# Two of four row blocks turned by VectorE and DMAs in the prologues of an attention and Fourier kernel

## The chip, the cores and the metric

The kernel runs on one core of a Trainium2 chip. The metric is the device time in microseconds of one execution. Before the change the median of three runs is 2447.65 us, the lowest 2446.1 and the highest 2448.53. A profiled execution of the same kernel took 2448.28 us. Its span, from the first to the last instruction, is 2446.5 us; all times inside the trace count from the span's start. The granted clock of TensorE was 0.998 of full speed over the span.

## The reference

The input x has 2048 rows (tokens) of 640 values in f32. Two kinds of block alternate, twice each, and each adds its result to x. An attention block normalizes every row, forms queries, keys and values with one 640 x 1920 matrix, runs 32 heads of 20 columns over all 2048 tokens with softmax, and multiplies with a 640 x 640 matrix. A Fourier block normalizes every row and takes the real part of a two-dimensional discrete Fourier transform, written as products with cosine and sine matrices.

```python
q, k, v = (x @ wqkv).reshape(B, S, 3, H, Dh) ...        # of the normalized x
p = softmax(einsum("bhqd,bhkd->bhqk", q, k) * Dh ** -0.5)
o = einsum("bhqk,bhkd->bhqd", p, v) ... @ wo
x = x + A(layernorm(x)); x = x + B(layernorm(x))         # and both once more
```

## The kernel before, in words

The kernel is written for the five engines with a schedule by hand: the order in which the code issues instructions is the order on each engine's queue. An engine works through its queue strictly in order, and a waiting instruction holds up all that stand behind it. SyncE (SP) and GpSimd (POOL) each have a queue of DMAs too. Tiles live in named pools: a tile that takes the place of an earlier one of the same tag waits until that one has been read.

There are two layers, each one attention block and one Fourier block. Each layer begins with a *prologue* (`Qkv.prologue`), and it is only this stage that the change touches. In it the rows of x are normalized, turned so that the 640 features lie on the partitions, and the first products are made from them: one 128-column chunk of queries, one of keys, and half of the value columns. After the prologue the attention proper begins, which holds most of the time.

The 2048 rows come in 16 tiles of 128 tokens. The prologue loads them in pairs, `k` = 0 to 7 (`load`, lines 148 to 153), and works in four *blocks* of 512 tokens, `tb` = 0 to 3; block `tb` holds the pairs 2 `tb` and 2 `tb` + 1. The steps of a block are these:

- `stats` (line 155): VectorE's statistics of a pair through `moments` (lines 114 to 129), and GpSimd's two small operations that make a scale and a bias of them (lines 127 and 128).
- `norm` (line 158): ScalarE applies these with `normed` (lines 131 and 132), in place.
- `turn` (lines 166 to 185): TensorE transposes the block against an identity, 4 tiles of tokens by 5 chunks of 128 features (`ND` is 5), into the PSUM tiles `ptr`. For each chunk, `split` (lines 85 to 91) makes the tile `xt` of two halves: ScalarE copies `ptr` into the high half, rounded to the type of TensorE's products; VectorE subtracts, which leaves the rest as the low half.
- the products of the block for the query and the key chunk, 15 matmuls each (`product`, through line 103: per chunk the high half, the low half, and the high half with the weights' low part), and `keep` (lines 200 to 225), which copies a product out, splits it the same way into `hl`, squares it for a bound, and has GpSimd write it to memory (`scrq`, `scrk`, line 224).
- `norms` (line 227), one small matmul `pn` and a maximum over it.
- `own` (line 339), four times: 15 matmuls make the values of one token tile (`pv`), and ScalarE copies them to `v` (line 265).

The loop over the blocks stands at the end of `prologue`. It is staggered: in block 0 the rows of block 2 are loaded, its statistics made and block 1's rows normalized. The values of block 0 are made ahead of `turn(1)`. In blocks 1 and 2 the next block is turned ahead of the values, so that ScalarE and VectorE split the chunks while TensorE works on `pv`. PSUM has eight banks, which the prologue's tiles take in turn.

On SyncE's queue stand, in order, the loads of x, a few small loads of `attention.setup` (line 495), the loads of the first queries (`qload`, lines 522 and 523), a load of weights (`fetch`, line 191) and those of the first keys (`kload`, lines 508 and 509). They serve the attention that follows, the weights a chunk of it. In the second layer the first block's rows are not loaded: `take` (line 285) normalizes them out of tiles of the Fourier block.

Of the kernel before, what the change touches and what calls it, by code (L numbers as in the profile page):

```python
# [5 lines left out]
F32 = mybir.dt.float32  # L6
F32R = mybir.dt.float32r
# [8 lines left out]
S, D, H, DH = 2048, 640, 32, 20  # L16
# [3 lines left out]
ND = D // 128  # L20
# [19 lines left out]
def mha_fnet_kernel(ctx, tc, x_in, wqk, wv, wo, seq, hid, nat_seq, nat_hid, out):  # L40
# [44 lines left out]
    def split(hl_h, hl_l, src, vector=False):  # L85

        if vector:
            V.tensor_copy(hl_h, src)  # L88
        else:
            A.activation(hl_h, src, AF.Copy)  # L90
        V.tensor_tensor(hl_l, src, hl_h.bitcast(F32), op=OP.subtract)  # L91
# [39 lines left out]
    def normed(dst, x, rs, i):  # L131
        A.activation(dst, x, AF.Identity, scale=rs[:, 0, i:i + 1], bias=rs[:, 1, i:i + 1])
# [5 lines left out]
    class Qkv:  # L138
        def __init__(s, L, src):
            s.L, s.src = L, src  # L140
            s.xn, s.xt, s.rs, s.v, s.sq = {}, {}, {}, {}, {}
            s.scr = {qk: dr.tile([D, 2, S], F32, name=f"scr{qk}_{L}") for qk in "qk"}
            s.shift = {n: dr.tile([H, 2, c], F32, name=f"shift{n}_{L}") for n, c in (("b", 512), ("m", S))}
            s.n = 1
            s.made, s.raw, s.silent = set(), {}, False


        def load(s, k):

            s.xn[k] = (s.first if k % 4 < 2 else s.room)(f"x{k % 4}", [2, D], F32, "xa")  # L150
# [15 lines left out]
        def turn(s, tb, wait=False):  # L166

            def transpose(p, i, dc):
                PE.transpose(p[:, i * 128:(i + 1) * 128],
                             s.xn[2 * tb + i // 2][:, i % 2, dc * 128:(dc + 1) * 128], ident)  # L170

            ps = [s.bank([128, 512], "ptr") for _ in range(ND if wait else 0)]
            for i in range(4 if wait else 0):
                for dc in range(ND):
                    transpose(ps[dc], i, dc)
            for dc in range(ND):
                if wait:
                    p = ps[dc]
                else:
                    p = s.bank([128, 512], "ptr")  # L180
                    for i in range(4):
                        transpose(p, i, dc)
                x = s.xtp(f"xt{tb}_{dc}", [2, 512], F32R, "xt")
                s.xt[tb, dc] = [x[:, 0], x[:, 1]]
                split(x[:, 0], x[:, 1], p)

        def fetch(s, c, room=None, tag="wraw", wait=False):
            s.raw[c] = (room or s.fill)(tag, [ND, 128], F32, "wraw")
# [83 lines left out]
        def begin(s, first, kq, vals, room, given):  # L272


            s.first, s.room, s.given, s.w = first, room, given, {}
            for k in range(2):
                if given:
                    s.raw[k * ND] = given.wraw[k]
                else:
                    s.load(k)  # L280
            s.wvraw = [vals(f"v{NT - 1 - dc}", [HD], F32, "wvraw") for dc in range(ND)]
            if given:
                s.load_values()

        def take(s, k):

            s.xn[k] = s.first(f"x{k}", [2, D], F32, "xa")
            for i in range(2):
                normed(s.xn[k][:, i], s.given.x[2 * k + i][:, 0], s.given.next[k], i)

# [4 lines left out]
        def prologue(s, vals, xt, fill, att):  # L295
# [39 lines left out]
            def later(tb, k, f):  # L335
                if tb + 2 < NB:
                    f(2 * tb + 4 + k)

            def own(tb, n, between=None):
                t = 4 * tb + n  # L340
                p = s.bank([128, HD], "pv")
                for dc in range(ND):
                    for f in s.value(p, t, dc):
                        f()
                    if between and dc == 1:
                        between()
                s.own(p, t, 0, False)

            for tb in range(NB):

                sq, late, last = {}, tb == 0, tb == NB - 1
                if late:
                    for k in range(2):
                        later(tb, k, s.load)
                for k in (1, 0) if last else (0, 1):
                    p = s.bank([128, 512], "pqk")
                    for dc in range(ND):
                        for f in s.product(p, s.w[k], tb, dc):
                            f()
                    sq[k] = s.keep(p, k * ND, tb, False, (room, fill)[k])  # L360
                    if late:
                        s.stats(2 + k)
                        continue
                    later(tb, k, s.stats)
                if late:
                    for n in range(4):
                        own(tb, n)
                        if n < 2:
                            s.norm(2 + n)
                            later(tb, n, s.stats)  # L370
                if tb == 0:
                    att.setup()
                elif tb == 1:
                    for t in range(NT - ND, NT):
                        ones(t)
                if tb + 1 < NB:
                    s.turn(tb + 1)
                    for k in range(2):
                        later(tb + 1, k, s.load)
                for k in range(1 if last else 0, 2):  # L380
                    later(tb, k, s.norm)
                    s.norms(s.bank, k * ND, tb, sq[k])
# [1261 lines left out]
```

## Time and profile before

| what | us |
|---|---|
| median of three runs | 2447.65 |
| lowest and highest | 2446.1, 2448.53 |
| the profiled execution | 2448.28 |
| its span | 2446.5 |
| TensorE busy in the span | 2423.7 |
| ScalarE busy | 2114.9 |
| VectorE busy | 996.3 |
| GpSimd busy | 530.7 |

In the profile PE is TensorE's matmuls, PEld its loads of weights, which run beside matmuls, DVE is VectorE, ACT is ScalarE, POOL is GpSimd and SP is SyncE; an engine's name with a q is its queue of DMAs. A group `xt<-ptr` writes the tile `xt` from the tile `ptr`. "L103" is line 103 of the kernel. A line like `29.43 2.56 ACT L90 ACTIVATE xt<-ptr ... x5` in a view in order of time means: from 29.43 us on, for 2.56 us, ScalarE ran five instructions of line 90. Its instructions overlap a little, so that the spacing from one to the next is shorter than one instruction's length. Brackets at the end of a line say how long the engine had been idle before it and what ended the wait.

### The profile page before, as it was taken

How to read it: one execution, taken by the hardware profiler on the slowest of the kernel's cores; microseconds unless marked ns; L12 is line 12 of the kernel's file. 1: busy time of each engine (PE TensorE's matmuls, PEld its weight loads, DVE VectorE, ACT ScalarE, POOL GpSimd, SP SyncE). 2: the span in 40 equal slices, each digit the busy share in tenths (PEclk: the TensorE clock that was granted, in tenths of full speed). 3: DMA queues.
4: the chain of work that ended last, by engine and by line, in shares of the span. 5: the costliest groups of instructions: out<-in, count | busy, mean ns of one | idle time of the engine just before them, and what ended most of it. 6: DMA issues, size and time to landing. Idle time of an engine off the chain costs nothing. (4 is left out here: it accounts for less than half of the span.)

```text
span 2446.5 us, 43831 instructions
## 1 busy us (share of the span) xinstructions
PE 2423.7 (99%) x16320; PEld 1167.8 (48%) x16320; DVE 996.3 (41%) x2250; ACT 2114.9 (86%) x2428; POOL 530.7 (22%) x1036
## 2 busy tenths in 40 slices
PE   8999999999999999999999999999999999999998
PEld 7644444443333332339885444454433333333496
DVE  6244442234343333428753444323433332333275
ACT  6699998899999999995457999988999999999862
POOL 2022211112212212115421212211111211222143
PEclk9999999999999999999999999999999999999999
DMA  5324231223232225318552332312221322252265
GB/s 186 101 88 127 83 111 53 77 69 111 73 95 90 87 89 164 98 38 293 196 181 96 112 102 86 117 54 70 78 82 57 93 63 69 57 153 79 77 240 198
DMA packets 128226, 262.63 MB, mean 107 GB/s; under 512 B 29936, under 2 KB 54288, under 8 KB 128004
## 3 DMA queue, kind: packets, MB, share of 16 engines
q1 hardware_dynamic: 89412, 159.89, 20.2%
q0 software_dynamic: 38592, 99.85, 12.8%
q8 instruction: 131, 2.15, 0.4%
q14 instruction: 91, 0.75, 0.1%
HBM read 175.29 MB, written 84.31 MB: 106 GB/s over the span
## 5 line engine op out<-in xcount | busy, mean ns | idle before, releaser
L547 ACT ACTIVATE e<-psc 128x1024 f32<-128x1024 f32 x2048 | 1917.3, 1060 | 108.8 <-PE psc L544 98.2
L555 PE MATMUL acc<-e,v 128*32 128x512 f32 x8192 | 1030.0, 600 | 0.4 <-DVE of L562 0.4
L544 PE MATMUL psc<-stq,stk 62*128 62x512 f32 x4096 | 746.7, 445 | 1.9 <-ACT e L547 0.5
L544 PEld LDWEIGHTS psc<-stq,stk 62*128 62x128 f32 x4096 | 334.2, 184 | 704.8 <-ACT e L547 567.7
L555 PEld LDWEIGHTS acc<-e,v 128*32 128x32 f32 x8192 | 211.0, 108 | 407.2 <-issue 369.7
L103 PE MATMUL pqk<-xt,wqk 128*128 128x512 f32 x1200 | 319.1, 407 | 0.4 <-DVE xt L91 0.4
L576 POOL DMA_DIRECT2D o<-oh x256 | 131.8, 523 | 825.0 <-DVE oh L571 813.1
L88 DVE CAST hl<-pqk 128x512 fp32r<-128x512 f32 x64 | 44.3, 692 | 603.7 <-PE pqk L103 603.7
L103 PEld LDWEIGHTS pqk<-xt,wqk 128*128 128x128 f32 x1200 | 213.2, 188 | 83.5 <-issue 39.5
L103 PE MATMUL pv<-wv,xt 128*128 128x320 f32 x960 | 151.7, 313 | 0.0
L103 PEld LDWEIGHTS pv<-wv,xt 128*128 128x128 f32 x960 | 141.0, 188 | 13.5 <-issue 9.7
L562 DVE STREAM_TRANSPOSE of<-acc 128x512 f32<-128x512 f32 x64 | 45.8, 715 | 225.3 <-PE acc L555 225.3
L576 POOL DMA_DIRECT2D o<-ot x256 | 128.2, 509 | 1.1 <-issue 0.8
L224 POOL DMA_DIRECT2D scrk<-hl x40 | 27.7, 693 | 412.3 <-DVE hl L91 251.9
L224 POOL DMA_DIRECT2D scrq<-hl x40 | 28.3, 707 | 405.5 <-DVE hl L91 239.9
L96 PE MATMUL py<-wo,o 128*128 128x320 f32 x320 | 101.0, 316 | 0.0
L825 DVE TENSOR_REDUCE far<-cq 128x1 f32<-128x512 f32 (+5 forms) x169 | 98.6, 584 | 5.7
L98 PE MATMUL py<-wo,o 128*128 128x320 f32 x320 | 98.8, 309 | 0.2 <-DMA o<-o 0.2
L97 PE MATMUL py<-wo,o 128*128 128x320 f32 x320 | 98.7, 308 | 0.0
L829 DVE TENSOR_TENSOR cq<-cq 128x512 f32<-128x512 f32 (+4 forms) x166 | 96.4, 581 | 4.6 <-DMA cq<-in_nat_seq_dram 3.3
L263 DVE COPY v<-pv 128x320 f32<-128x320 f32 x32 | 15.7, 490 | 161.2 <-PE pv L103 161.2
L233 DVE TENSOR_REDUCE top<-pn 32x1 f32<-32x512 f32 x50 | 33.7, 676 | 76.6 <-PE pn L232 76.5
(204 smaller groups left out, 1761.9 us busy)
## 6 DMA issues: line engine op xcount, KB each, us to landing
cq<-in_nat_seq_dram POOLq DMA_DIRECT2D x64, 512.0 KB, 5.3
scrq<-hl POOLq DMA_DIRECT2D x40, 512.0 KB, 3.3
scrk<-hl POOLq DMA_DIRECT2D x40, 512.0 KB, 3.1
stq<-scrq SPq DMA_DIRECT2D x256, 80.0 KB
stk<-scrk SPq DMA_DIRECT2D x128, 160.0 KB
o<-o SPq DMA_DIRECT2D x32, 384.0 KB
stq<-scrq SPq DMA_DIRECT2D x256, 40.0 KB
stk<-scrk SPq DMA_DIRECT2D x128, 80.0 KB
```

The costliest lines, as they stand in the source:

```text
L96: PE.matmul(out_ap, ah, bh, start=start, stop=False)
L97: PE.matmul(out_ap, ah, bl, start=False, stop=False)
L98: PE.matmul(out_ap, al, bh, start=False, stop=stop)
L103: yield lambda i=i, j=j, k=k: PE.matmul(out_ap, a[i], b[j], start=dc == 0 and k == 0, stop=dc == ND - 1 and k == 2)
L224: G.dma_start(s.scr["qk"[k]][c * 128:(c + 1) * 128, :, tb * 512:(tb + 1) * 512], hl.bitcast(F32))
L544: PE.matmul(p[:, i], s.k[g, kc // 8, j][r, kc % 8 * 128:(kc % 8 + 1) * 128], s.q[g, qb, j][r], start=True, stop=True)
L547: A.activation(e, p, AF.Exp, scale=SCALE)
L555: PE.matmul(s.acc[32 * j:32 * j + 32], s.a.v[kc][:, v0:v0 + 32], s.e[n, j // 2][:, j % 2], start=kc == 0, stop=kc == NT - 1, skip_group_ch ...
L562: V.transpose(t0.rearrange("p b c -> p (b c)"), s.acc)
L576: G.dma_start(s.o[k, h * DH:(h + 1) * DH, qb * 512:(qb + 1) * 512], hl[k][32 * j:32 * j + DH])
L825: V.tensor_reduce(to, x, op=OP.max, axis=AX.X, apply_absolute_value=True)
L829: V.tensor_tensor(y, x, y, op=op)
```

## The change

Blocks 0 and 1 are turned as before. Blocks 2 and 3 of each layer are no longer transposed by TensorE. In place of `norm` and `turn` they go through three new steps:

- `spaced` normalizes a pair's two token tiles, not in place but into a tile `y` (`xs`) of four slots. A slot `g` takes, of every chunk of 128 features, the 32 features 32g to 32g + 31. So each row of 640 values is written in 20 runs of 32.
- `swap` runs VectorE's transpose of 32x32 pieces over each slot (128 partitions by 640 values), into four tiles `z` (`xz`) in the room of the values' tiles v12 to v15. Then 16 DMAs bring every group of 32 partitions of each `z` to its place: partitions 32i to 32i + 31 of tile `z` number g go to partitions 32g to 32g + 31, slot i, of `y`. Each moves 32 rows of 2560 bytes, 80 KB. Those of g = 0 and 1 stand on SyncE's queue, those of g = 2 and 3 on GpSimd's.
- `unspaced` splits the five chunks out of `y` into the high and low halves of `xt`, as `turn` did out of PSUM. ScalarE copies and VectorE subtracts, both now from SBUF.

The order of the work around them changes too. In block 0 the statistics of block 2's pairs follow as before, and `spaced(4)` comes after the third value tile; after `turn(1)` come the loads of the last rows, then `norms`, `spaced(5)` and `swap(2)`, all ahead of `qload`. In block 1 `unspaced(2)` comes after the second value tile, `spaced(6)` follows it, `spaced(7)` and `swap(3)` come after the third. In block 2 `unspaced(3)` comes after the second value tile. The ones written into the value tiles v12 to v15 (`ones`) move from block 1 to after this.

The tiles of x are merged, two pairs in one (`tiles`): `x0` holds the pairs 0 and 1, or 4 and 5, and `x2` the pairs 2 and 3, or 6 and 7. Block 2's `y` lies in the room of block 3's `xt`, block 3's `y` in that of the pairs 4 and 5.

```diff
+        def tiles(s, k):
+            if k % 2 == 0:
+                s.xb = (s.room if k % 4 else s.first)(f"x{k % 4}", [4, D], F32, "xa")
+            s.xn[k] = s.xb[:, 2 * (k % 2):2 * (k % 2) + 2]
...
+        def spaced(s, k):
+            tb, j = divmod(k, 2)
+            if j == 0:
+                s.y[tb] = s.xtp("xt3_0", [4, ND, 4, 32], F32, "xs") if tb == 2 else s.first("x0", [4, ND, 4, 32], F32, "xs")
+            for i in range(2):
+                x = s.xn[k][:, i].rearrange("p (c g f) -> p g c f", c=ND, g=4)
+                normed(s.y[tb][:, :, :, 2 * j + i], x, s.rs[k], i)
+
+        def swap(s, tb):
+            zs = [s.vals(f"v{NT - 1 - g}", [ND * 128], F32, "xz") for g in range(4)]
+            for g, z in enumerate(zs):
+                V.transpose(z, s.y[tb][:, g].rearrange("p c n f -> p (c n f)"))
+            for g, z in enumerate(zs):
+                for i in range(4):
+                    (nc.sync if g < 2 else G).dma_start(s.y[tb][32 * g:32 * g + 32, i].rearrange("p c n f -> p (c n f)"), z[32 * i:32 * i + 32])
+
+        def unspaced(s, tb):
+            y = s.y[tb].rearrange("p i c n f -> p c i n f")
+            xs = [s.xtp(f"xt3_{i}", [ND // 2 + 1 - i, 2, 512], F32R, "xt") for i in range(2)] if tb == 3 else None
+            for dc in range(ND):
+                x = xs[dc > ND // 2][:, dc % (ND // 2 + 1)] if xs else s.xtp(f"xt{tb}_{dc}", [2, 512], F32R, "xt")
+                s.xt[tb, dc] = [x[:, 0], x[:, 1]]
+                split(*[x[:, k].rearrange("p (n i f) -> p i n f", n=4, i=4) for k in range(2)], y[:, dc])
...
                         if n < 2:
                             s.norm(2 + n)
-                            later(tb, n, s.stats)
+                            s.stats(4 + n)
+                        elif n == 2:
+                            s.spaced(4)
                 if tb == 0:
                     att.setup()
                 elif tb == 1:
-                    for t in range(NT - ND, NT):
+                    for t in range(NT - ND, NT - 4):
                         ones(t)
-                if tb + 1 < NB:
-                    s.turn(tb + 1)
+                if late:
+                    s.turn(1)
                     for k in range(2):
-                        later(tb + 1, k, s.load)
+                        s.load(6 + k)
                 for k in range(1 if last else 0, 2):
-                    later(tb, k, s.norm)
                     s.norms(s.bank, k * ND, tb, sq[k])
+                if late:
+                    s.spaced(5)
+                    s.swap(2)
...
                     for n in range(4):
                         own(tb, n, bounds if last and n == 0 else None)
+                        if n == 1 and not last:
+                            s.unspaced(tb + 1)
+                            if tb == 2:
+                                for t in range(NT - 4, NT):
+                                    ones(t)
+                        if n in (1, 2) and tb == 1:
+                            s.spaced(5 + n)
+                        if n == 2 and tb == 1:
+                            s.swap(3)
```

More of the change, by code (lines that the diff above doesn't have):

```diff
@@ L140, in __init__ @@
             s.L, s.src = L, src
-            s.xn, s.xt, s.rs, s.v, s.sq = {}, {}, {}, {}, {}
+            s.xn, s.xt, s.rs, s.v, s.sq, s.y = {}, {}, {}, {}, {}, {}
             s.scr = {qk: dr.tile([D, 2, S], F32, name=f"scr{qk}_{L}") for qk in "qk"}
@@ L145, in __init__ @@
             s.made, s.raw, s.silent = set(), {}, False
+        def tiles(s, k):
+            if k % 2 == 0:
+                s.xb = (s.room if k % 4 else s.first)(f"x{k % 4}", [4, D], F32, "xa")
+            s.xn[k] = s.xb[:, 2 * (k % 2):2 * (k % 2) + 2]
         def load(s, k):
-            s.xn[k] = (s.first if k % 4 < 2 else s.room)(f"x{k % 4}", [2, D], F32, "xa")
+            s.tiles(k)
             n = 1 if k < 2 else 2
@@ L272, in begin @@
         def begin(s, first, kq, vals, room, given):
-            s.first, s.room, s.given, s.w = first, room, given, {}
+            s.first, s.room, s.given, s.w, s.vals = first, room, given, {}, vals
             for k in range(2):
@@ L285, in take @@
         def take(s, k):
-            s.xn[k] = s.first(f"x{k}", [2, D], F32, "xa")
+            s.tiles(k)
             for i in range(2):
```

## The prediction

> **What bounds the kernel now.** I read the busy totals first, then the two prologues in order of time, then the prices of single instructions.
>
> ```profile
> PE 2423.7 (99%) x16320; PEld 1167.8 (48%) x16320; DVE 996.3 (41%) x2250; ACT 2114.9 (86%) x2428; POOL 530.7 (22%) x1036
> ```
>
> TensorE is busy for 2423.7 of 2446.5 us, so time is saved only where TensorE has less to do, and lost only where it is made to wait. The transposes that the change removes, by stretch and for the tile `ptr` alone (columns: length, then each engine's time in it, TensorE first):
>
> ```profile
> 38.10:41.00 2.90, 2.34 (x20) 2.24 (x20) 0.00 (x0) 1.45 (x4) 1.00 0.88 298
> 56.44:59.26 2.82, 2.34 (x20) 2.24 (x20) 0.16 (x1) 1.38 (x3) 1.00 0.49 186
> 1250.56:1253.39 2.83, 2.35 (x20) 2.25 (x20) 0.00 (x0) 1.38 (x3) 1.00 0.88 292
> 1268.89:1271.71 2.82, 2.34 (x20) 2.24 (x20) 0.16 (x1) 1.38 (x3) 1.00 0.49 186
> ```
>
> Four groups of 20 transposes, 2.34 or 2.35 us each. TensorE has no gap around them, so what is taken out shortens the prologue unless something else comes late. The order of time in layer 0 (start, length, engine, line; in brackets what the engine had waited for):
>
> ```profile
> 28.31 0.20 POOL L128 TENSOR_TENSOR ars<-ars 128x2 f32<-128x2 f32 x1
> 28.80 2.35 PE L169 MATMUL ptr<-ident,xa 128*128 128x128 f32 x20
> 29.00 0.44 ACT L265 ACTIVATE v<-pv 128x320 f32<-128x320 f32 x1 [0.72 <-PE pv L103]
> 29.43 2.56 ACT L90 ACTIVATE xt<-ptr 128x512 fp32r<-128x512 f32 x5
> 30.06 3.08 DVE L91 TENSOR_TENSOR xt<-ptr,xt 128x512 fp32r<-128x512 f32 x5
> 31.39 7.10 PE L103 MATMUL pqk<-xt,wqk 128*128 128x512 f32 x30
> 31.84 3.38 ACT L132 ACTIVATE xa<-xa,ars 128x640 f32<-128x640 f32 x4
> 32.00 0.92 SPq L522 DMA_DIRECT2D stq<-scrq  x1
> 37.62 0.38 SPq L191 DMA_DIRECT2D wraw<-in_wqk_dram  x1
> 38.33 2.34 PE L169 MATMUL ptr<-ident,xa 128*128 128x128 f32 x20
> 40.77 0.88 DVE L121 BATCH_NORM_STATS2 ast<-xa 128x6 f32<-128x320 f32 x2
> 40.93 9.07 PE L103 MATMUL pv<-wv,xt 128*128 128x320 f32 x60
> ```
>
> and, from a later stretch,
>
> ```profile
> 43.13 3.07 DVE L91 TENSOR_TENSOR xt<-ptr,xt 128x512 fp32r<-128x512 f32 x5
> 44.92 0.28 SPq L508 DMA_DIRECT2D stk<-scrk  x1
> 49.83 7.00 PE L103 MATMUL pqk<-xt,wqk 128*128 128x512 f32 x30
> ```
>
> The reader is to see three chains. ScalarE copies the five chunks of block 1 out of PSUM from 29.43, 0.51 us apart, VectorE subtracts from 30.06, 0.62 apart, TensorE starts the product at 31.39: the first chunk's high half (ScalarE) is ready over a microsecond ahead, its low half (VectorE) at 30.06 + 0.68 = 30.74, wanted one matmul later, at 31.62. VectorE's pair of statistics takes 40.77 to 43.13, 2.36 us. SyncE issues the query loads from 32.00 to 37.6 and stands idle until 44.92. The same place in layer 1:
>
> ```profile
> 1241.24 0.74 ACT L265 ACTIVATE v<-pv 128x320 f32<-128x320 f32 x2
> 1241.63 0.19 POOL L128 TENSOR_TENSOR ars<-ars 128x2 f32<-128x2 f32 x1
> 1241.88 2.54 ACT L90 ACTIVATE xt<-ptr 128x512 fp32r<-128x512 f32 x5
> 1243.34 3.08 DVE L91 TENSOR_TENSOR xt<-ptr,xt 128x512 fp32r<-128x512 f32 x5
> 1243.71 7.24 PE L103 MATMUL pqk<-xt,wqk 128*128 128x512 f32 x30
> 1250.79 2.35 PE L169 MATMUL ptr<-ident,xa 128*128 128x128 f32 x20
> ```
>
> Here there is no cover: the copies begin at 1241.88, the subtractions at 1243.34 and the product at 1243.71, with 7.24 us for its 30 matmuls where layer 0 needs 7.10.
>
> **The change part by part.** *Removed.* 80 transposes, 2.34 + 2.34 + 2.35 + 2.34 = 9.37 us of TensorE. ScalarE's copies and VectorE's subtractions of these chunks stay, with a source in SBUF instead of PSUM.
>
> *Added and moved.* The prices, each from the view of its tile or line (least, median and longest in ns; under it the time from a DMA's issue to its landing), the first for the tile `ot`, then for lines 224, 90 and 508, and the copies of v by shape (busy us, mean ns):
>
> ```profile
> L576 POOL DMA_DIRECT2D o<-ot x256: 505/505/842, 125.0 to 2319.1; - x128
> L569 DVE STREAM_TRANSPOSE ot<-on x64: 711/711/715, 121.4 to 2314.1; 128x512 f32<-128x512 f32 x64
> L572 DVE TENSOR_TENSOR ot<-ot,oh x64: 691/693/694, 122.6 to 2315.3; 128x512 f32<-128x512 f32 x64
> DMA to landing us min/median/max: 1.8/2.0/6.0
> ```
> ```profile
> L224 POOL DMA_DIRECT2D scrq<-hl x40: 673/700/908, 20.2 to 2126.6; - x40
> DMA to landing us min/median/max: 3.1/3.2/7.8
> ```
> ```profile
> L90 ACT ACTIVATE wv<-wvraw x10: 454/470/473, 16.0 to 1229.9; 128x320 fp32r<-128x320 f32 x10
> L90 ACT ACTIVATE wqk<-wraw x4: 720/736/741, 9.6 to 1212.8; 128x640 fp32r<-128x640 f32 x4
> ```
> ```profile
> L508 SPq DMA_DIRECT2D stk<-scrk x128: 272/274/1173, 44.9 to 2188.4; - x128
> ```
> ```profile
> L265 ACT ACTIVATE v<-pv 128x320 f32<-128x320 f32 x16 | 6.8, 434 | 18.8 <-PE pv L103 18.8
> ```
>
> (a) `spaced` writes a normalized 128x640 row tile in runs of 32 elements. At the spacing of 31.84 it is 3.38/4 = 0.85 us. No row shows runs of 32; bounds: 0.85 below, and above twice that, 1.7. I take 0.85, since the nearest row, the copy of v in runs of 20 (434 ns for 320 elements), is no dearer than a contiguous copy of 320 (470).
>
> (b) Its place. The first pair, `spaced(4)`, stands on ScalarE ahead of the last copy of v of block 0 and of block 1's five copies out of PSUM. In layer 0 its scales are ready at 28.31 + 0.20 = 28.5, so it runs to 30.2, v's copy to 30.6, the first copy of block 1 to 31.2, the first subtraction to 31.9, wanted at 31.62: TensorE loses 0.3 us. In layer 1 its scales are ready at 1241.63 + 0.19 = 1241.8; it runs to 1243.55, v's copy to 1243.95, the first copy of block 1 to 1244.55, the first subtraction to 1245.25, where it ended at 1243.34 + 0.68 = 1244.0: TensorE loses 1.25 us. Bounds: 0 in both if ScalarE is earlier than I think, and at 1.7 us a tile 1.7 more in each layer, 5.0 in all. Behind the copies two norms remain of the four at 31.84, so ScalarE is back in step by 35.
>
> (c) The 32x32 transposes: four a block on VectorE, 640 elements each. From 711 ns for 512, 711 x 640/512 = 0.89 us; bounds 0.71 and 1.1. They need the second pair, `spaced(5)`, at 33.2 + 1.7 = 34.9 in layer 0, when VectorE has just done block 1's subtractions, and run to 38.5. Behind them wait the query product's subtraction, both pairs of statistics, the key product's maximum and subtraction and the reduction of `pn`: 38.5 + 0.7 + 2.36 + 0.4 + 0.7 + 2.36 + 0.7 = 45.7. Then VectorE is free for block 2.
>
> (d) Sixteen DMAs of 80 KB a block. SyncE's eight cost 0.3 to 0.4 us each (274 ns, 0.38 at 37.62), GpSimd's eight 0.51 (505 ns for 20 rows, 700 for 256; 32 lie near the first). GpSimd's first needs the third transpose, 37.6, or all four, 38.5, so its eighth goes out between 41.2 and 42.1. Landing takes 2.0 us (40 KB) or 3.2 (512 KB), at worst 6.0 and 7.8; 80 KB lies near 2.0. All have landed by 44.1.
>
> (e) What queues behind them. On SyncE the query loads of 32.00, the weight load of 37.62 and the key loads of 44.92: now 40.1 to 45.7, 46, and 48 to 51. The loads serve the scores after the whole prologue, the weights VectorE after block 2's product; nothing waits. On GpSimd the write of the query product (now about 43) and the scales of rows 6 and 7 (44.2 and 46.2); these are wanted by `spaced(6)`, which stands behind block 2's copies, after 46.
>
> (f) Block 2's split. Its product began at 49.83 and begins 2.34 - 0.3 earlier, 47.8 (high half), 48.0 (low half). ScalarE copies after the second tile of v, at 43.8, and after the landing, 44.1. From SBUF a copy of 512 lies between 470 and 736 ns, 0.63 by proportion, and the subtraction with both sources in SBUF is 693. With VectorE free at 45.7 the first chunk is ready at 46.4, the later ones every 0.69 us, and TensorE takes one in 0.70. Spare: 1.6 us by VectorE, and 48.0 - 0.63 - 0.69 - 44.1 = 2.6 for the landing. In layer 1 the same sums give transposes until 1251.8, landing by 1257.4, product at 1261.2: 2.7.
>
> (g) Block 3. `spaced(7)` ends at 51, the transposes at 54.5, GpSimd's last issue at 57.8, landing 59.8; TensorE wants the block at 63.8: 2.9 spare by the sum of (f), 2.6 in layer 1. The cover is v's four tiles (9.07 us at 40.93); without it (c) and (d), some 9 us a block, would be TensorE's wait.
>
> (h) The merged tiles of x make the load of row tiles 4 wait for all of block 0's transposes, and in layer 1 the first `take` wait for the room of both halves:
>
> ```profile
> 1214.49 1.73 ACT L132 ACTIVATE xa<-xd,ars 128x640 f32<-128x640 f32 x2
> 1217.23 1.73 ACT L132 ACTIVATE xa<-xd,ars 128x640 f32<-128x640 f32 x2
> ```
>
> No row shows who held the second half; between nothing and 1217.23 - 1214.49 = 2.7 us. I take nothing, since each earlier owner is of a finished stage. The ones of v's last tiles move to a place where GpSimd is idle.
>
> Sum: 9.37 - 0.3 - 1.25 = 7.8 us gained. The profiled execution took 2448.28 us (span 2446.5 and 1.8 around it), so 2440.5; the median of the runs is 0.63 below that execution, so 2440.
>
> [...] GpSimd's issue beside VectorE's copies:
>
> ```profile
> 124.95 2.00 POOL L576 DMA_DIRECT2D o<-ot  x4
> ```
> ```profile
> 125.86 0.32 DVE L88 CAST wv<-wvraw 128x320 fp32r<-128x320 f32 x1
> ```
>
> Four DMAs took 2.00 us with a copy among them, 0.50 each: no lengthening is seen. [...]
>
> **Rivals.** *1. The row tiles are dear on ScalarE* (1.7 us each, part b): 9.37 - 5.0 = 4.4 us, 2443. For it: no row shows runs of 32. Against: runs of 20 cost nothing.
>
> *2. GpSimd's issue is drawn out* by VectorE's work: each DMA at 1.02 us, twice the median (the longest is 0.84). The eight then end 4.1 later and the spares of 2.6, 2.7, 2.9 and 2.6 leave 1.5 + 1.4 + 1.2 + 1.5 = 5.6 us of waiting: net 2.2, 2445.5. Against it: the 2.00 us above.
>
> *3. The other side: landing is late.* The transfers go from SBUF to SBUF, which no large one of this trace does, beside the query loads and the products' writes. If the last lands 7.8 us after issue (the longest row) instead of 2.0, TensorE waits 3.2 + 3.1 + 2.9 + 3.2 = 12.4: a loss of 4.6, 2452. The change breaks even when landing is 4.65 us later than I have it (4 x 4.65 - 10.8 = 7.8), and is slower by 0.2% from 5.9. For it: both longest landings are 6 us or more. Against: the medians, 2.0 and 3.2.
>
> *4. The full gain*: ScalarE's order costs nothing, 9.37 us, 2438.
>
> **How the numbers follow.** 0.2%, 4.9 us, is about what a measurement of this kernel can tell from no change. Forecast 2440, chance 0.54, with its own range 2438.5 to 2442; rival 4, 0.08; rival 1, 0.12; rival 2, 0.08; rival 3, 0.18. Faster by over 0.2% means under 2442.7: the forecast, rival 4 and a quarter of rival 1, 0.65. Within 0.2%: the rest of rival 1, rival 2 and a third of rival 3, 0.22. Slower: the rest of rival 3, 0.13. The range holds the forecast, rivals 4, 1 and 2 and the mild end of 3: 2437.5 to 2449.
>
> **What would show it.** Right: block 1's product followed at once by the small `pn` matmul and v, only 40 `ptr` transposes a layer, the products of blocks 2 and 3 beginning without a wait, layer 1's block 1 product about 1.2 us later than its transposes allow. Wrong: TensorE waiting for `xt` at the head of product 2 or 3 behind a ScalarE that waits for the DMAs into `xs` (rivals 2 and 3, told apart by the length of GpSimd's issues), or `spaced` instructions near 1.7 us (rival 1). What would break the argument altogether is a VectorE transpose of 1.3 us or more, since 1.6 us is all that its queue can spare for four.

## The result, with the profile after

The kernel after takes 2441.86 us in the median of 13 runs (2440.42 to 2446.45), beside 2447.65 of the kernel before in 13 runs (2446.1 to 2449.0). The ratio is 0.9978, with a 95% interval of 0.9969 to 0.9987. That is 5.8 us faster, where 7.8 was forecast. A second measurement of the same two kernels, on another chip, gave 4.2 us (experiment 5). The profiled execution of after took 2446.45 us (span 2444.7) and is the slowest of its 13, so its trace shows more waiting than the median execution can have.

The page of after, busy time and the group of the query and key products, and last the same group on the page of before:

```profile
PE 2415.6 (99%) x16240; PEld 1158.4 (47%) x16240; DVE 1008.1 (41%) x2266; ACT 2115.4 (87%) x2428; POOL 547.7 (22%) x1068
L103 PE MATMUL pqk<-xt,wqk 128*128 128x512 f32 x1200 | 320.3, 407 | 5.2 <-ACT xt L90 3.8
L103 PE MATMUL pqk<-xt,wqk 128*128 128x512 f32 x1200 | 319.1, 407 | 0.4 <-DVE xt L91 0.4
```

TensorE does 80 matmuls less (16320 before), but the products now wait for `xt`: 5.2 us instead of 0.4. The view in order of time, TensorE alone, layer 0 (start, length, group, count; in brackets the idle time before and what ended it):

```profile
28.77 2.35 PE L175 MATMUL ptr<-ident,xa 128*128 128x128 f32 x20
32.05 6.90 PE L103 MATMUL pqk<-xt,wqk 128*128 128x512 f32 x29 [0.18 <-DVE xt L91]
39.20 9.06 PE L103 MATMUL pv<-wv,xt 128*128 128x320 f32 x60
48.09 6.99 PE L103 MATMUL pqk<-xt,wqk 128*128 128x512 f32 x30
55.33 9.06 PE L103 MATMUL pv<-wv,xt 128*128 128x320 f32 x60
65.93 0.49 PE L103 MATMUL pqk<-xt,wqk 128*128 128x512 f32 x1 [1.54 <-ACT xt L90]
66.66 6.85 PE L103 MATMUL pqk<-xt,wqk 128*128 128x512 f32 x29 [0.23 <-DVE xt L91]
73.75 1.14 PE L103 MATMUL pv<-wv,xt 128*128 128x320 f32 x6
83.85 1.06 PE L590 MATMUL psc<-stq,stk 62*128 62x512 f32 x6 [0.53 <-ACT v L298]
85.54 0.50 PE L590 MATMUL psc<-stq,stk 62*128 62x512 f32 x2 [0.63 <-ACT e L593]
```

and layer 1:

```profile
1244.15 0.50 PE L103 MATMUL pqk<-xt,wqk 128*128 128x512 f32 x1 [1.18 <-ACT xt L90]
1260.92 6.99 PE L103 MATMUL pqk<-xt,wqk 128*128 128x512 f32 x30
1277.96 0.49 PE L103 MATMUL pqk<-xt,wqk 128*128 128x512 f32 x1 [0.74 <-ACT xt L90]
1295.88 1.05 PE L590 MATMUL psc<-stq,stk 62*128 62x512 f32 x6 [0.53 <-ACT v L298]
```

Block 1's product is followed by `pn` and v at 39.20, not by transposes, and block 2's product at 48.09 waits for nothing. Three waits are new: block 1's product in layer 1 (1.18 us), block 3's in both layers (1.54 and 0.74), and the first scores (0.53 us, and 0.63 where before had 0.25). The view of instructions by tile, for what was added:

```profile
L132 ACT ACTIVATE xs<-xa,ars x16: 903/912/956, 28.7 to 1263.2; 128x640 f32<-128x640 f32 x16
L206 DVE STREAM_TRANSPOSE xz<-xs x16: 790/802/845, 34.9 to 1266.4; 128x640 f32<-128x640 f32 x16
```

and by line; the last two rows are the time from issue to landing, first of block 2's DMAs and then of block 3's, both of layer 0:

```profile
L209 SPq DMA_DIRECT2D xs<-xz x32: 507/563/642, 35.7 to 1271.7; - x32
L209 POOL DMA_DIRECT2D xs<-xz x32: 498/511/813, 37.8 to 1271.3; - x32
DMA to landing us min/median/max: 2.1/2.9/3.1
DMA to landing us min/median/max: 6.0/6.1/6.3
```

Durations are in ns, the landing in us, each as least, median and most. The view gives the landing of GpSimd's DMAs alone. In layer 1 its medians are 2.7 us in block 2 and 5.2 in block 3, so block 3's DMAs take about twice as long as block 2's; the median of all 32 together, 4.1, belongs to neither. A row tile of `spaced` lasts 0.91 us by itself (two take 1.73, below), a VectorE transpose 0.80, a DMA 0.56 us of SyncE's queue and 0.51 of GpSimd's. The prologue's other side in order of time, layer 0:

```profile
28.73 1.73 ACT L132 ACTIVATE xs<-xa,ars 128x640 f32<-128x640 f32 x2 [0.27 <-POOL ars L128]
35.75 5.23 SPq L209 DMA_DIRECT2D xs<-xz  x8
37.79 4.01 POOL L209 DMA_DIRECT2D xs<-xz  x8 [6.70 <-DVE xz L206]
44.83 2.71 ACT L90 ACTIVATE xt<-xs 128x512 fp32r<-128x512 f32 x5 [0.50 <-DMA stq<-scrq]
53.59 6.56 SPq L209 DMA_DIRECT2D xs<-xz  x8
54.12 3.98 POOL L209 DMA_DIRECT2D xs<-xz  x8 [8.40 <-DMA stk<-scrk]
61.13 0.73 POOL L257 DMA_DIRECT2D scrq<-hl  x1 [3.03 <-DMA xs<-xz]
65.05 0.17 POOL L363 MEMSET v<- 128x32 f32 x1 [0.85 <-DMA xs<-xz]
65.25 2.71 ACT L90 ACTIVATE xt<-xs 128x512 fp32r<-128x512 f32 x5 [4.78 <-DMA scrq<-hl]
```

Block 2's DMAs go out from 35.75 on and ScalarE copies at 44.83. Block 3's go out from 53.59 on, and ScalarE copies only at 65.25, 11.7 us after the first issue. The bracket of that copy names another DMA that ended near. That block 3's own DMAs are what it waits for shows in the line above it: GpSimd writes ones into the room of `z` when these DMAs have read it, and the last of these waits ends at 65.05.

To compare executions I cut a layer's prologue into four stretches, from start to start of TensorE's groups. A runs to block 1's values (`pv`), in layer 0 from block 1's transposes and in layer 1 from block 0's product. B runs from there to block 2's values, C to block 3's, D to the first filler product between the scores. The first column has before's length in microseconds, the others what a trace gained against it. "Again" is a second profiled execution of the same kernel; the repairs are those of experiments 1 to 3, together.

| stretch | before | after | after, again | three repairs | three repairs, again |
|---|---|---|---|---|---|
| layer 0 A | 12.13 | 1.70 | 1.63 | 2.19 | 2.19 |
| B | 18.33 | 2.20 | 2.19 | 2.19 | 2.20 |
| C | 16.14 | -2.28 | -1.56 | 0.01 | -1.62 |
| D | 11.58 | -0.64 | -0.63 | 0.00 | 0.01 |
| layer 1 A | 29.37 | 0.43 | 1.29 | 3.44 | 2.74 |
| B | 18.32 | 2.19 | 2.19 | 2.19 | 2.18 |
| C | 16.13 | -1.50 | -1.44 | -0.98 | -1.04 |
| D | 11.58 | -0.62 | -0.63 | 0.00 | 0.00 |
| sum | | 1.48 | 3.04 | 9.04 | 6.66 |

The sums answer to the spans, which are 1.8, 3.2, 9.3 and 6.8 us below 2446.5. So all but 0.1 to 0.3 us of the change's effect lies in the prologues.

### The profile page after: what moved, and what is told of

Read it like the earlier page. It is cut to its first block, busy times and chain, and to the rows that moved or that the text cites. A ratio compares the mean times of both kernels' runs of the same rounds, so it can differ in the third digit from the quotient of the medians.

```text
span 2444.7 us, 43845 instructions
## 1 busy us (share of the span) xinstructions
PE 2415.6 (99%) x16240; PEld 1158.4 (47%) x16240; DVE 1008.1 (41%) x2266; ACT 2115.4 (87%) x2428; POOL 547.7 (22%) x1068
```

## The experiments

All are edits of the kernel after. Ratios are against the kernel before, run beside them on the same chip: 2447.07 us in the median for experiments 1 to 4, 2447.53 for 5, 6, 8 and SyncE alone in 7, and 2447.74 for 9, 10, GpSimd alone in 7 and the second measurement of 4.

**1. The scores' bank.** In D the first scores wait 0.53 us for `v`, that is for ScalarE's last copy out of the PSUM bank they take over. With ten PSUM tiles fewer in the prologue the kernel's cycle through eight banks (`s.n % 8`) ends two further back.

```diff
-            s.n = 1
+            s.n = 3
```

> The counter of PSUM banks starts at 3 instead of 1, so that the last tile of v lies in the bank where it lay before the change (ten transposed tiles fewer are 2 modulo 8). Theory: the changed kernel's first scores wait for ScalarE's copy of that tile, 0.53 us and 0.6 more at the following step, in each layer; with the old bank 2 x 0.63 = 1.3 us come back, median 2440.6. Rival: ScalarE's copy holds up the first exponential anyway, and nothing comes back: 2441.9.

Measured 2442.24 us (2440.01 to 2445.78), ratio 0.9979 [0.997, 0.9988]. In order of time, the first scores of its trace in layer 0, and the step after them in the trace of before:

```profile
84.72 1.40 PE L590 MATMUL psc<-stq,stk 62*128 62x512 f32 x6
86.55 0.50 PE L544 MATMUL psc<-stq,stk 62*128 62x512 f32 x2 [0.25 <-ACT e L547]
```

The first scores no longer wait, the step after them waits 0.25 us as before, and D is back at before's 11.58 to within 0.01 in both layers. The cause of D's 1.26 us is shown by the trace; the median, which came out 1.6 above the forecast, can't resolve it. In this execution block 3's product waited 1.76 us in layer 0 and C lost 4.16 (last section).

**2. The place of `spaced(4)`.**

```diff
-                        elif n == 2:
-                            s.spaced(4)
...
                 if late:
+                    s.spaced(4)
                     s.spaced(5)
```

> spaced(4) moves on ScalarE's queue to behind block 1's copies out of PSUM, directly ahead of spaced(5). Theory: its old place cost TensorE 0.55 us in layer 0 and 1.86 in layer 1; both come back, 2.4 us, so the median is 2439.5, and the first VectorE transpose starts at the same time as now (34.9 in layer 0) because ScalarE's work up to it is the same. Rival: the transposes come later by the moved 1.7 us and block 2's product waits instead: no gain, 2441 to 2443.

Measured 2443.41 us (2439.11 to 2447.89), ratio 0.9983 [0.9974, 0.9992]. A gains 2.19 in both layers, so ScalarE's order is what it loses otherwise, and B still gains 2.2, so block 2's product doesn't wait. The median shows none of this; it lies above the theory and the rival. In this execution block 3's product in layer 0 waited 3.49 us, and stretch C lost 5.87. The DMAs went out later than in after, against the expectation: block 2's first at 36.93 (35.75) and block 3's at 55.49 (53.59). How much of the 3.49 us comes of that is open.

**3. The key loads ahead of block 3's DMAs.** Eight loads of keys stand on SyncE from 50.38 to 53.3 us, right ahead of the first DMA of block 3.

```diff
                     s.fetch(ND + 1)
-                    for j in range(2):
-                        att.kload(0, 0, j)
...
                             s.swap(3)
+                            for j in range(2):
+                                att.kload(0, 0, j)
```

> The eight key loads move on SyncE's queue from ahead of block 3's eight DMAs to behind them. Theory: these 960 KB ahead of them are why block 3's DMAs land late in the profiled execution. Then TensorE no longer waits at the head of block 3's product (2.3 us in layer 0 and 1.7 in layer 1 of the changed kernel's trace), the profiled execution is about 4 us faster, near 2442.5, and the median, which seems to hold little of this wait, stays between 2440.5 and 2442. Rival: the sixteen transfers themselves are slow, since the DMA engines are full at some 240 GB/s: then a wait of at least 1 us remains in both layers and the profile stays above 2444.

Measured 2442.36 us (2440.64 to 2443.51), ratio 0.9979 [0.997, 0.9988]. Layer 0's block 3 waits for nothing (C 0.01), layer 1's loses 1.09, so the theory holds in one layer and the rival in neither. The landing of GpSimd's DMAs of block 3 in layer 0 is now:

```profile
DMA to landing us min/median/max: 2.0/2.6/3.9
```

That is 2.6 us in the median instead of 6.1, and in layer 1 2.7 (at most 5.4) instead of 5.2. The other traces agree. With the key loads ahead (experiments 1, 2, 5 and 8) the median is 5.8 to 7.2 us in layer 0 and 4.1 to 6.6 in layer 1; with them behind (4 and 9) it is 2.6 to 2.9 and 2.7 to 4.2. So the key loads ahead of them are a cause of the slow landing. They aren't all of it: the copies still begin 9.9 and 12.3 us after the first issue (11.7 and 12.3 in after), and the median of the runs isn't lower.

**4. The three together.**

> The three edits together. Theory: the losses lie at different places and add: 2.4 + 1.3 us off the median, 2438.2, and the profiled execution near it (2438.5 to 2439.5), as no wait for block 3 is left. That is the whole 9.37 us of the transposes. Rival: the places are linked (an earlier block 1 leaves block 2's chain with less cover) and the median stays above 2439.5.

Measured 2440.05 us (2438.43 to 2443.03), ratio 0.997 [0.9959, 0.9982]. The profiled execution, 2438.95, is as forecast; the median is the rival's, above 2439.5. A second time, on another chip:

> The kernel with the three repairs once more, on this call's chip, beside the one that turns block 3 earlier: 2440.0 (2439.2 to 2441.0) by what it gave before. Its profile says in which of its waits the next execution differs: by the theory of the late landing only block 3's product may wait, by less than a microsecond, in one layer or both.

2440.93 us (2438.8 to 2443.54), ratio 0.9973 [0.9962, 0.9984]. A and D come back as the table shows; in layer 1 A gains more than the 2.19 us of the transposes because those of block 1 don't wait for their rows here, as they did in before (0.39 + 0.48 us, see b below). Both medians lie below every other kernel's here, but the intervals overlap with that of after. As forecast only block 3's product waits, 0.85 and 0.28 us. In the second trace A, B and D gain 9.3 us together and C gives 2.7 back. Its lines in order of time, layer 0:

```profile
52.18 5.24 SPq L209 DMA_DIRECT2D xs<-xz  x8
57.52 0.45 SPq L553 DMA_DIRECT2D stk<-scrk  x1
64.13 2.71 ACT L90 ACTIVATE xt<-xs 128x512 fp32r<-128x512 f32 x5 [4.09 <-DMA xs<-xz]
64.81 0.50 PE L103 MATMUL pqk<-xt,wqk 128*128 128x512 f32 x1 [0.85 <-ACT xt L90]
```

The copies start 12 us after the first issue, though the key loads now stand behind it. TensorE asks for block 3 at 63.96 here, 0.4 us earlier than in after (64.39): the repairs ahead of it give part of their gain back as a wait.

**5. The kernel after once more.**

> The changed kernel again, unchanged, for a second trace of it. Theory: TensorE's wait at the head of block 3's product is a matter of when the DMAs happen to land, and differs from execution to execution; this trace shows it with another size in at least one layer (2.3 and 1.7 us in the first), while the wait at the first scores (0.53 us and the 0.38 more that follows) and the 9 us from block 2's first issue to its copies are the same. The median is 2441 to 2443. Rival: the waits are fixed by the order of issue and come out within 0.2 us of the first trace.

Measured 2443.37 us (2441.15 to 2446.84), ratio 0.9982 [0.9973, 0.9992]. That is 4.2 us below before's 2447.53 and 0.4 above the expected range. C differs from execution to execution in layer 0, where block 3's product now waits 0.76 us instead of 1.54, and A differs in layer 1; D doesn't. The rival is out.

**6. Block 3's DMAs left out.**

```diff
-            for g, z in enumerate(zs):
+            for g, z in enumerate(zs if tb == 2 else []):
                 for i in range(4):
```

> Block 3's sixteen DMAs are left out, so that its rows are turned only within their 32x32 pieces; everything else runs. Theory: the median execution holds some wait for these DMAs, 1 to 2 us over both layers, and it goes; ScalarE's order (0.3 to 0.5 and 1.3 to 1.9) and the PSUM bank (1.3) stay. Median 2440 to 2441, and its runs lie closer together than those of the changed kernel (2440.4 to 2446.5), at about the 2.9 us of the kernel before. Rival: the median holds no such wait: 2441.9 with the same spread.

Measured 2441.65 us (2440.88 to 2445.3), ratio 0.9978 [0.9968, 0.9987]. C is 0.01 and -0.01 in its trace, as it must be. Beside it on the same chip after took 2443.37 (experiment 5), which is 1.7 us more, as the theory has it; against after's first median, 2441.86 on another chip, it is 0.2, as the rival has it. The intervals overlap, so what block 3's landing costs the median execution lies between 0.2 and 1.7 us and isn't settled. The runs spread over 4.4 us, where after's spread over 5.7 (experiment 5) and 2.9 was expected. So the landing makes only a part of the spread. One other part shows in the traces: block 0's first product, ahead of all that the change touches, differs in length (here it put block 1's transposes off by 0.6 us; see also experiment 10).

**7. One queue instead of two.** First all sixteen DMAs of a block on SyncE, then all on GpSimd.

```diff
-                    (nc.sync if g < 2 else G).dma_start(
+                    nc.sync.dma_start(
```

In the second kernel `G.dma_start(` stands there.

> All sixteen DMAs of a block on SyncE's queue, in place of eight there and eight on GpSimd's. SyncE's issue of one measures 0.56 us, so sixteen take 9 us where eight took 5.2, and the last goes out at about 45 in block 2 of layer 0 and 62 in block 3. Theory: issue time bounds the landing; the copies start near 48 and 66.5, TensorE waits some 1.5 us at block 2 and 2 to 4 more at block 3 in each layer, median 2446 to 2452. Rival: the DMA engines bound it, at some 240 GB/s whoever issues: within 1 us of the changed kernel, 2441 to 2443.

> All sixteen DMAs of a block from GpSimd, none from SyncE. Theory A (with SyncE alone the loss came from SyncE's issue, 0.70 to 0.80 us for each of sixteen, and what stands behind it): GpSimd issues sixteen at 0.50 us, 8 us, behind the fourth transpose; block 2's copies start 3 us later than in the kernel after (48 in layer 0), its product waits some 1 us in each layer, block 3's 1 to 3 with the slow matmuls behind it; 2446 (2444 to 2450). Theory B (one queue lands as slowly whichever it is): as with SyncE alone, 2458 or more.

SyncE alone: 2462.51 us (2460.97 to 2465.02), ratio 1.0059 [1.0043, 1.0075], against an expected 2446 to 2452. GpSimd alone: 2454.3 us (2452.52 to 2455.85), ratio 1.0029 [1.0018, 1.004], between the ranges of the two theories. The issues in order of time, of the first kernel:

```profile
35.18 11.29 SPq L209 DMA_DIRECT2D xs<-xz  x16
56.29 12.72 SPq L209 DMA_DIRECT2D xs<-xz  x16
```

and of the second:

```profile
43.76 0.50 POOL L209 DMA_DIRECT2D xs<-xz  x1 [1.50 <-DMA xs<-xz]
58.19 6.35 POOL L209 DMA_DIRECT2D xs<-xz  x13 [0.71 <-DVE hl L256]
```

SyncE takes 0.71 and 0.80 us for each of sixteen, where it takes 0.65 for each of eight beside GpSimd's. GpSimd issues at 0.50, but its thirteenth waited 1.50 us for an earlier one to land. With GpSimd alone theory A's waits came true (block 2's copies at 48.07, its product late by 0.81 and 0.44 us, block 3's by 2.52 and 2.73), but it put too little on them: C lost 4.73 and 4.92 where it has 1 to 3, since the matmuls behind such a wait run slower (last section), 8.3 us for 29 instead of 6.9. With SyncE alone the waits were 1.77 and 1.53 us at block 2 and 3.52 and 5.62 at block 3, whose 30 matmuls then took 10.00 and 9.68. So in this kernel the second queue is worth 11 us beside GpSimd alone and 19 beside SyncE alone (against 2443.37 of experiment 5), more than the transposes.

**8. Another split of the queues.** SyncE gets the destination groups 0 and 2, GpSimd 1 and 3.

```diff
-                    (nc.sync if g < 2 else G).dma_start(
+                    (nc.sync if g % 2 == 0 else G).dma_start(
```

> The queues share the sixteen DMAs another way: SyncE takes the groups of destination partitions 0 to 31 and 64 to 95, GpSimd 32 to 63 and 96 to 127. The number of DMAs on each queue and their bytes stay. Theory A: which partitions are written at one time does not matter; landing as now, 9 us from the first issue in block 2, median 2441 to 2443. [...]

Measured 2446.42 us (2444.64 to 2450.77), ratio 0.9995 [0.9985, 1.0004]: 3.05 us worse than after in experiment 5, on the same chip. GpSimd's landing took 3.2 us in the median in block 2 in both layers, instead of 2.9 and 2.7, and 6.7 and 6.6 in block 3 instead of 6.1 and 5.2. From 54 to 65 us the DMA engines moved 223 GB/s at a share of 1.02, where after moved 251 at 0.94. So theory A's median, 2441 to 2443, is missed, and in this trace the landing is slower with the new split. For the start of the copies that is little: in layer 0 they started 9.57 us after the first issue in block 2 (9.08 in after) and 12.33 in block 3 (11.66), some half a microsecond later, and in layer 1 8.86 (9.25) and 12.43 (12.26). C lost 4.00 and 4.29, and part of that is the slower product of the last section, 1.6 us each: behind the waits of 1.63 and 1.87 us the 29 matmuls took 8.47 and 8.51, behind after's 1.54 and 0.74 they took 6.85. What makes this split slower isn't shown: there is one trace, of the slowest of this kernel's executions.

**9. Block 3 turned earlier** (with the three repairs): `spaced(6)` and `spaced(7)` ahead of block 2's copies, `swap(3)` right behind these.

```diff
+                        if n < 2 and tb == 1:
+                            s.spaced(6 + n)
                         if n == 1 and not last:
                             s.unspaced(tb + 1)
...
-                        if n == 2 and tb == 1:
+                        if n == 1 and tb == 1:
                             s.swap(3)
```

> The three repairs together, and block 3 turned earlier: its two normalizations stand ahead of block 2's copies, and its four transposes, its sixteen DMAs and then the eight key loads right behind those copies. Theory (what is left of the spread of the kernel with the three repairs is the time at which block 3's DMAs land): the first of the sixteen is issued at some 51 us instead of 53.6, the copies start by 60 us in layer 0 and by 1272 in layer 1, block 3's product waits in neither layer, and the median is 2438.8 (2438.0 to 2439.8), the whole 9.37 us of the transposes less what block 2 still loses. Rival (the rest is not the landing): the median stays at 2440 or above, though block 3's products wait for nothing. Second rival: the work put ahead of block 2's copies makes those late, and block 2's product waits a microsecond or more.

Measured 2441.86 us (2439.35 to 2445.47), ratio 0.9977 [0.9968, 0.9986]. The second rival came true. ScalarE in order of time:

```profile
45.38 1.74 ACT L132 ACTIVATE xs<-xa,ars 128x640 f32<-128x640 f32 x2 [2.28 <-POOL ars L128]
49.07 2.70 ACT L90 ACTIVATE xt<-xs 128x512 fp32r<-128x512 f32 x5
```

`spaced(6)` waits 2.28 us for GpSimd's scales, which stand behind its eight DMAs, so block 2's copies start at 49.07 instead of 44.98, B loses 1.3 and 0.7 us, and block 3's first DMA goes out at 53.64, no earlier than in after. Whether an earlier start helps was thus not tested.

**10. Block 2 alone**, block 3 by TensorE.

```diff
+                if tb == 2:
+                    s.turn(3)
                 for k in range(1 if last else 0, 2):
+                    if tb == 1:
+                        s.norm(6 + k)
                     s.norms(s.bank, k * ND, tb, sq[k])
...
-                        if n == 1 and not last:
+                        if n == 1 and tb == 1:
...
-                        if n in (1, 2) and tb == 1:
-                            s.spaced(5 + n)
-                        if n == 2 and tb == 1:
-                            s.swap(3)
```

The counter of experiment 1 stands at 6.

> Block 2 alone by VectorE and DMAs; block 3 by 20 transposes of TensorE in each layer as before the change, and the PSUM counter set so that the first scores find a free bank. Theory (block 3's half is worth little in the kernel after: its transposes' 4.69 us go against late landing, halved clock and bank waits): removed 2.34 and 2.35 us; lost by ScalarE's order 0.1 to 0.5 us in layer 0 and 0.1 to 1.9 in layer 1; median 2444.0 (2443.0 to 2445.3), and a smaller spread than the kernel after has, since no wait for block 3 is left. Rival (block 3's half is worth nothing or less at all): 2442 or below, no slower than the kernel after.

Measured 2446.9 us (2446.27 to 2448.37), ratio 0.9998 [0.9989, 1.0007]: no gain that can be told, 2.9 us above the expectation. Neither theory holds, but the spread is smaller as expected, 2.1 us. Its trace names three losses:

```profile
12.38 9.55 PE L103 MATMUL pqk<-xt,wqk 128*128 128x512 f32 x30
44.38 1.74 ACT L132 ACTIVATE xa<-xa,ars 128x640 f32<-128x640 f32 x2 [2.94 <-POOL ars L128]
48.70 2.71 ACT L90 ACTIVATE xt<-xs 128x512 fp32r<-128x512 f32 x5
1224.54 1.97 PE L175 MATMUL ptr<-ident,xa 128*128 128x128 f32 x16 [1.16 <-DVE top L336]
```

A gained 2.19 and 2.59. B lost 0.57 and 1.13, since the normalization of rows 6 and 7, again ahead of block 2's copies, waits for the scales and puts the copies off to 48.70. The counter that I had set to 6 put layer 1's first transposes on a bank still being read, 1.16 us (the wait ends at 1224.5, with VectorE's last read of the tile `phid`; the bracket names the instruction behind that read). And block 0's first product, ahead of all that was edited, took 9.55 us, after which layer 0's block 1 transposes began at 30.57 instead of 28.80; the traces of three other kernels show 0.6 to 1.4 us of this too, and its cause is open. So this median isn't block 2's worth by itself: two of the losses came with my edit. In the stretches block 2's half, A, gave 4.8 us, and normalizing block 3's rows ahead of block 2's copies took 1.7 of it back in B, as it took 2.0 in experiment 9. What the other half is worth stands in B, C and D of the table: 4.4 us, less a wait that differs by execution and less the scores' bank.

## Why the prediction was right, and where its sizes were off

The direction and the mechanism were right: the removed transposes shorten the prologue, and the medians lie in the stated range (2437.5 to 2449). That the first median lies in the forecast's own range (2438.5 to 2442) is in part luck: it is 0.14 us inside, the second, 2443.37, is outside, and errors of both signs went into it. By its steps:

- **(a) `spaced`, right.** 1.73 us for two tiles, 0.87 each where 0.85 was taken; rival 1 is out.
- **(b) its place, right on average.** Forecast losses were 0.3 and 1.25. Without the loss stretch A would gain the 2.19 of the transposes. In the nine traces that keep this order it lost 0 to 0.56 in layer 0 (mean 0.2), and in layer 1 between a gain of 0.4 and a loss of 1.92 (mean 0.97). In layer 1 the stretch holds a second wait, which this order doesn't set. There block 1's transposes wait for their normalized rows, in before:

```profile
1240.58 0.33 PE L169 MATMUL ptr<-ident,xa 128*128 128x128 f32 x1 [0.39 <-ACT xa L132]
1241.39 2.07 PE L169 MATMUL ptr<-ident,xa 128*128 128x128 f32 x17 [0.48 <-ACT xa L132]
```

  In the nine traces this takes from none to 1.17 + 0.48 us. Counted from `pn`, behind these transposes, to block 1's values (10.00 us in before), the loss is 0.97 to 1.64, in the mean 1.2, close to the forecast. Where `spaced(4)` was moved (experiments 2, 4 and 9) 0.12 to 0.68 of it is left.
- **(c) VectorE's transposes, a little dear:** 0.80 each against 0.89.
- **(d) the DMAs, wrong for SyncE and for the landing.** SyncE takes 0.56 a piece (0.65 from one to the next), not 0.3 to 0.4. GpSimd's 0.51 was right, and its issue was hardly drawn out beside VectorE's work (eight in 4.01 us, and in 3.98 where the copy of the weight split began at 57.95 beside the last of them; one DMA of the 32 took 0.81), so rival 2 is out: the 1.02 us that it takes for one DMA is shown by no run. GpSimd's landing took 2.0 us in neither block: 2.9 and 2.7 in block 2, 6.1 and 5.2 in block 3.
- **(e) right:** `scrq` stood 3.03 us behind the landing (61.13), and TensorE waited for none of what queues there. That the same scales hold up whatever is put ahead of block 2's copies was seen only in experiments 9 and 10 (waits of 2.28 and 2.94 us).
- **(f) block 2, right:** copies at 44.83 for 44.1, no wait in either layer of after. The spare of 2.6 took up the later landing.
- **(g) block 3, the step that failed.** It was to land at 59.8 and be wanted at 63.8. The first DMA went out at 53.59, behind the eight key loads, which ended at 53.3 instead of 51. SyncE's last issue ended at 60.15, where the last of all was to go out at 57.8, and the copies began at 65.25, 5.1 us behind it instead of 2.0. So of the 5.45 us by which the block was late 2.35 are issue and 3.1 landing. While the DMAs were under way the transfers went slowly, by the view of stretches (the last two columns are the busy share of the DMA engines and what they moved):

```profile
33.00:35.00 2.00, 2.00 (x11) 1.61 (x10) 2.00 (x5) 1.84 (x3) 0.00 (x0) 1.00 1.01 393
55.00:63.00 8.00, 8.00 (x54) 7.76 (x54) 2.93 (x5) 1.96 (x4) 4.97 (x10) 1.00 0.98 240
```

  At a full share 240 GB/s went through where 393 did earlier. That is rival 3, mild, with a wait of 1.54 + 0.23 and 0.74 + 0.23 us in this execution. The sign that the prediction names for it, TensorE waiting at the head of product 3, is there in both layers; what was missed is that the key loads just ahead slow the landing (experiment 3). Each trace of a kernel that shares block 3's DMAs between the queues shows another wait, from none to 3.49.
- **(h) right:** from D's end in layer 0 to block 0's product in layer 1 it is 1137.12 us, and 1137.04 in before, so the merged tiles cost nothing that shows.
- **The term that was missing:** the scores' PSUM bank, 0.64 and 0.62 (D). Ten PSUM tiles fewer shift the banks of all that follows.
- **The gain itself was 0.6 too large.** A removed group of transposes gives 2.19 or 2.20 us from start to start (B), not its length of 2.34, since it overlaps its neighbours: 8.8 in all, not 9.37.
- **In the chances** two sums are off by 0.01: the terms give 0.23 within 0.2% and 0.12 for slower. Nothing hangs on it.

So the median's 5.8 is, as an estimate from the traces, 8.8 - 1.2 (the means of A's losses in both layers) - 1.26 (D) = 6.3, less what block 3's wait costs on average; that leaves 0.5 us for it, and 2.1 by the second measurement's 4.2. The key loads are a cause of the late landing; what else makes it differ from one execution to the next stays open. In four of the nine measurements whose block 3 uses both queues the profiled execution is the slowest, so profiling itself may delay the landing; this wasn't tried.

## What to carry to other kernels

Count a removed group from start to start of its neighbours, and when tiles leave a rotation of buffers, look at which buffer the next stage begins. A transfer's spare is to be checked against everything else that moves in its stretch, with the landing times of that stretch and not the medians of the whole trace: 2.0 us was taken for a landing that took 6.1 and 5.2 in block 3. And what is put ahead of a late copy on the same engine must not itself wait for something later: here that cost 2.0 us in both layers together (experiment 9), almost as much as a group of transposes (2.19).

## What the runs showed of the hardware

A TensorE wait can cost twice. After the waits at the head of a product the 29 matmuls behind took 6.85 us in after (wait 1.54) but 8.3 to 8.5 in kernels that waited 1.63 to 3.49. In order of time, of experiment 1's kernel:

```profile
65.75 0.49 PE L103 MATMUL pqk<-xt,wqk 128*128 128x512 f32 x1 [1.76 <-ACT xt L90]
66.48 8.49 PE L103 MATMUL pqk<-xt,wqk 128*128 128x512 f32 x29 [0.23 <-DVE xt L91]
```

and by stretch, PEclk third from the end:

```profile
64.00:67.00 3.00, 1.01 (x3) 0.66 (x4) 1.26 (x3) 1.93 (x4) 0.66 (x8) 1.00 0.80 311
67.00:68.00 1.00, 1.00 (x4) 0.79 (x4) 1.00 (x3) 1.00 (x3) 0.00 (x0) 0.57 0.07 29
68.00:70.00 2.00, 2.00 (x7) 1.54 (x6) 0.84 (x2) 0.43 (x2) 0.00 (x0) 0.50 0.00 0
70.00:71.00 1.00, 1.00 (x5) 0.82 (x4) 0.00 (x0) 0.00 (x0) 0.00 (x0) 0.72 0.05 16
71.00:74.00 3.00, 3.00 (x15) 2.46 (x14) 1.12 (x2) 1.09 (x2) 0.23 (x1) 1.00 0.00 0
```

After 1.76 us of waiting the granted clock was halved for 3.4 us (a share of 0.86 of the second row, the third, and 0.56 of the fourth), and 1.6 us was lost. The product was as slow after waits of 1.63 (8.47 us), 1.77 (8.37), 1.87 (8.51), 2.52 and 2.73 (8.3) and 3.49 (8.48); after those of 1.63 and 3.49 the views by stretch show a granted clock of 0.50 too. After waits of 1.53 and 1.54 the product kept its length, and after the 1.54 the clock stayed at 1.00. So in these traces the edge lies between 1.54 and 1.63 us. They are few, and whether the length of the wait alone decides isn't shown. Where a wait differs from one execution to the next, as block 3's does (1.54 and 0.76 us in layer 0 of after), crossing this edge adds 1.6 us at once, which may widen the spread.
